# Layer 1 of a routed MLP in batches of four: seven products with 256 streamed columns instead of fourteen with 128

## The chip, the cores and the metric

The kernel runs on one core of a Trainium2 chip. Time is device time in microseconds (us) of one execution, of which the median over runs counts. The engines have short names in the profile: PE (TensorE, matmuls), PEld (its weight loads), DVE (VectorE), ACT (ScalarE), POOL (GpSimd) and SP (SyncE, which here only issues DMAs).

## The reference: what is computed

Attention with pooled queries for 8 batches of 8 heads, and then, in each batch, an MLP on the 128 tokens that score highest:

```python
q_pool = q.reshape(B, H, S // 2, 2, D).mean(axis=3)           # 8, 8, 576, 64
scores = q_pool @ k.transpose / sqrt(D); attn = softmax(scores)
x = (attn @ v) as (B, 576, 512)
scores = x @ w_gate
for b in range(B):
    top = the 128 tokens of batch b with the highest scores
    h = np.maximum(x[b, top] @ w1, 0.0)          # 512 -> 1024
    ye = h @ w2                                  # 1024 -> 512
    out[b, top] = x[b, top] + sigmoid(scores[b, top])[:, None] * ye
```

All of it is in float32.

## The kernel before, in words

The attention is one long loop of 64 half pairs (a pair is two heads of one batch, a half is 288 of its queries), and PE alternates between scores (`scores`, L878) and weighted values (`weighted`, L896). The other engines sum the exponentials, divide, multiply by `w_gate` and store the rows `x`.

In each batch a generator, `routed`, picks the tokens. Its steps are: add the parts of the scores (`line`, L1076, DVE), collect and add them up (`side_by_side` on ACT, `added` on DVE), write the row to DRAM and read it back shifted (L1088 and L1091, SP), compare every token's score with all others (L1116, DVE, ten instructions on `pick`), write the ranks to DRAM and read them back as a table (L1139 and L1143, SP), search in it for the tokens' numbers (L1152, DVE), gather their rows (L1179, a POOL DMA) into `xe`, and turn the gathered rows by way of DRAM (L1191 and L1209, SP) and a DVE transposition (L1216) into `xeT`, features on partitions. A `yield` stands between the steps, and the caller decides behind which other work each step is issued. Each engine takes its instructions in the order in which the code issues them.

The MLP of all batches is done behind the attention, in `ending` (L1383). Batches go in pairs, each pair in four stages. Two batches' tokens are taken as the two block rows of one matrix, the weight as 2 x 2 blocks, and each layer is done in seven block products instead of eight, with sums of blocks ahead of and behind them:

- `input_sums` (L1250): four sums of input blocks on POOL, 256 columns each (2 feature chunks of 128 tokens).
- `first_layer` (L1291): seven products of layer 1. `product(1, ...)` (L1263, matmuls at L1270) does one: eight matmuls, in each of which the weight block of 128 x 128 is stationary and the 128 tokens of one batch are streamed. Behind each product stand an ACT copy, or DVE adds (`add`, L1289) and a ReLU on ACT (L1303), 512 columns each. `u` and `w` are its two running sums.
- `four_sums` (L1344): four sums of blocks of the hidden layer on DVE, at L1351.
- `second_of` (L1353): seven products of layer 2 (matmuls at L1280; the tokens are stationary and 256 columns of the weight are streamed), adds on DVE, the gated residual (`scaled`, L1284), and `written` (L1238), which scatters a batch's rows to the output by a DMA of POOL.

The last pair's layer 2 is written out by hand in `ending`, with batch 7's scatter ahead of batch 6's.

The order of `ending` is this. Its first lines finish the attention. Batch 6's routing is under way (the generator `old`), batch 7's begins there (`new`). Then come the four pairs: layer 1, layer 2, layer 1, and so on. The steps that are left of `old` and `new` are issued by `pieces` (L1390): it counts the pieces of the MLP, of which each product is one, and before the pieces whose number is in `behind` it issues one step of the routing. So a step stands on its engines behind the work of the piece before.

Memory is taken over from the attention: `exponents_room`, `values_room` and `sums_room` are its buffers of exponentials, values and sums. PSUM is a pool of four buffers of two banks each (`banks`, L1063); they are handed out in turn, for products of either layer alike, so that a product waits until the work behind the fourth product before it has read its buffer.

Of the kernel before, what the change touches and what calls it, by code (L numbers as in the profile page):

```python
# [11 lines left out]
P = 128  # L12
# [3 lines left out]
F32 = mybir.dt.float32  # L16
# [524 lines left out]
class _Plain:  # L541
# [524 lines left out]
    def routed(self, b, part):  # L1066
# [16 lines left out]
        n = P - 1 + Sp  # L1083
# [61 lines left out]
        for s0, w in self.slots:  # L1145
# [27 lines left out]

            yield True
            if b == self.B - 1:
                xe = self.late[:, self.Dm : 2 * self.Dm]
# [16 lines left out]
            )  # L1193
            if b != self.B - 2:
                search(lines[:, :, 1, :], own_gate)
            if b < self.paired:
                xeT = ffn.tile([P, self.ND, P], F32, name="xeT", bufs=self.paired)
            else:
                xeT = self.lines_of((self.early if b < self.B - 1 else self.late)[:, 0 : self.Dm])
            yield True  # L1200
            moved = []

            def read():
                if b == self.B - 2:
                    moved.append(self.early[:, self.Dm : 2 * self.Dm])
                else:
                    room = ffn.tile([P, NT, P], F32, name="pick", bufs=1)
                    moved.append(room.rearrange("p t n -> p (t n)")[:, 0 : self.Dm])
                nc.sync.dma_start(moved[0], copy.rearrange("a (j b) m -> (a j) (b m)", b=n))  # L1209

            if b < self.B - 2:
# [8 lines left out]
            token = {"xe": xe, "xeT": xeT, "gate": own_gate, "index": index, "rows": rows_out, "w": w, "b": b}  # L1220
            self.tokens.append(token)

    def part_of_rows(self, token, part, parts):
# [36 lines left out]
    def lines_of(self, room):  # L1260
        return room.rearrange("p (c n) -> p c n", n=P)

    def product(self, layer, of, by, to):  # L1263

        n = of.shape[1]
        if layer == 1:
            to = self.lines_of(to)[:, :, 0 : of.shape[2]]
            for f in range(by.shape[2] // P):
                for k in range(n):
                    self.nc.tensor.matmul(  # L1270
                        to[:, f, :],
                        lhsT=by[:, k, f * P : (f + 1) * P],
                        rhs=of[:, k, :],
                        start=k == 0,
                        stop=k == n - 1,
                    )
        else:
            to = to[0 : of.shape[2], 0 : by.shape[2]]
            for k in range(n):
                self.nc.tensor.matmul(to, lhsT=of[:, k, :], rhs=by[:, k, :], start=k == 0, stop=k == n - 1)  # L1280
        return to

    def scaled(self, to, of, token, plus):
        self.nc.vector.scalar_tensor_tensor(  # L1284
# [5 lines left out]

    def first_layer(self, a, s, c, m):  # L1291

        copy = self.nc.scalar.copy
# [4 lines left out]
        def product(of, by):  # L1298
            return self.product(1, of, by, self.banks()[:, 0, :])

        def hidden(to, x, y):
            self.add(to, x, y)
            self.nc.scalar.activation(to, to, AF.Relu)  # L1303

        copy(u, product(a11, b11))
        yield
        hidden(c11, u, product(a12, b21))
        yield
        copy(w, product(s1, t1))
        yield  # L1310
        self.add(u, u, product(s2, t2))
        self.add(w, w, u)
        yield
        ps = product(s3, t3)
        hidden(c22, w, ps)
        self.add(u, u, ps)
        yield
        hidden(c21, u, product(a22, t4))
        yield
        hidden(c12, w, product(s4, b22))  # L1320
        yield

    def second_layer(self, a, s, order):

        (a11, a12, _, a22), (s1, s2, s3, s4) = a, s
        b11, b21, b22 = (self.quarter(2, i, j) for i, j in ((0, 0), (1, 0), (1, 1)))
        t1, t2, t3, t4 = self.last_sums
        products = (a11, b11), (a12, b21), (s1, t1), (s2, t2), (s3, t3), (s4, b22), (a22, t4)
        for i in order:
            yield self.product(2, *products[i - 1], self.banks()[:, 0, :])  # L1330
# [5 lines left out]
    def quarters_of(self, tiles, w):  # L1336

        n = tiles[0].shape[1] // 2
        return [tile[:, i * n : (i + 1) * n, 0:w] for tile in tiles for i in range(2)]
# [13 lines left out]
    def second_of(self, tokens, a, s, y):  # L1353

        copy, add = self.nc.scalar.copy, self.add
        half, w = self.Dm // 2, tokens[0]["w"]
        y1, y2, y7, y3, y4 = (y[0:w, i * half : (i + 1) * half] for i in range(5))
        to = [token["xe"][0:w, i * half : (i + 1) * half] for token in tokens for i in range(2)]
        one, two = tokens
        products = self.second_layer(a, s, (1, 2, 7, 3, 4, 5, 6))  # L1360
        for part in (y1, y2, y7):
            copy(part, next(products))
            yield
        copy(y3, next(products))
# [12 lines left out]
        for of, at, token in ((y3, to[1], one), (y4, to[2], two), (y7, to[3], two)):  # L1377
            self.scaled(at, of, token, at)
        for token in tokens:
            self.written(token, token["index"])  # L1380
        yield

    def ending(self, halves, old):  # L1383

        nc, half, copy = self.nc, self.Dm // 2, self.nc.scalar.copy
        last = halves[-1]["pair"]
        n, w = self.NFC * P, self.tokens[0]["w"]
        done, behind = 0, (8, 9, 10, 11, 15, 16, 17, 18, 23, 28, 29, 31, 32, 38)

        def pieces(unit, n=None):  # L1390
            nonlocal done
            for i, _ in enumerate(unit):
                if done in behind:
                    next(waiting)
                done += 1
                if i + 1 == n:
                    break

# [6 lines left out]
        def sums_room():  # L1405
            return self.row(self.work.tile([P, G, 2 * self.HALF], F32, name="acc"))

        def layers(i, room, m):
            tokens = self.tokens[2 * i : 2 * i + 2]
            c = self.quarters_of([self.lines_of(room[:, k * n : (k + 1) * n]) for k in range(2)], w)  # L1410
            s = self.lines_in(room[:, 2 * n : 4 * n], self.NFC // 2, w, 4)
            a = self.quarters_of([token["xeT"] for token in tokens], w)
            sums = self.lines_in(room[:, 4 * n :], self.ND // 2, w, 4)
            return tokens, c, s, (a, sums), self.first_layer(a, sums, c, m)

        self.early = values_room()
        rooms, acc = [exponents_room()], [sums_room(), sums_room()]
        m = [self.lines_in(acc[0], 4, w, 2)]
        m.append(self.lines_in(self.load.tile([P, self.S], F32, name="kT"), 4, w, 2))
        following = layers(0, rooms[0], m[0])  # L1420

        self.gated(halves[-3])
        next(old)
        self.weighted(halves[-1])
        self.drained(halves[-1])
        self.multiplied(halves[-2])
        self.input_sums(*following[3])
        self.multiplied(halves[-1])
        self.scored(halves[-3])
        self.gated(halves[-2])  # L1430
        self.late = values_room()
        rooms.append(exponents_room())
        pieces(following[4], 1)
        self.normalized(last)
        self.gated(halves[-1])
        self.scored(halves[-1])
        _, new, _ = self.routing.pop()
        waiting = chain((None for _ in old), (None for _ in new), count())
        pieces(following[4], 1)
        for of in (halves[-3]["pair"], last):  # L1440
            self.divided(of)
            self.stored(of)

        for i in range(1, self.B // 2):
# [10 lines left out]
        (six, seven), c, s, _, third = following  # L1455
        pieces(third, 3)
# [225 lines left out]
```

## Time and profile before

| What | us |
|---|---|
| Median of 3 runs (674.3 to 675.34) | 674.61 |
| The profiled execution's own time | 675.29 |
| Its span, first to last instruction | 673.6 |
| PE busy in the span | 665.6 |
| First product of layer 1 starts on PE | 568.67 |
| First product of the last pair's layer 2 starts | 655.65 |
| Last scatter is issued | 668.76 |

Times in the profile's views are us from the span's start, so the last 105 us of the table are the MLP. A line of the timeline has start, length, engine, line in the code, operation, output and input with their shape, the number of instructions, and in square brackets how long the engine was idle before and what it waited for. fp32 matmuls have two records each on PE, so that the eight matmuls of a layer 1 product are shown as x16. The granted TensorE clock is 1.0.

Of the stretches between 568.7 and 643.0 (columns: busy us of each engine with the number of instructions, PE's clock, DMA share, GB/s):

```profile
568.70:593.80 25.10, 25.10 (x176) 23.58 (x173) 16.66 (x34) 6.97 (x17) 8.90 (x11) 1.00 0.25 53
593.80:618.40 24.60, 24.60 (x170) 23.02 (x169) 18.20 (x46) 5.25 (x11) 5.54 (x8) 1.00 0.19 64
618.40:643.00 24.60, 24.60 (x171) 23.09 (x170) 15.07 (x28) 5.18 (x10) 6.06 (x7) 1.00 0.17 55
```

The order is PE, PEld, DVE, ACT, POOL. PE has no idle time in any of the three, and DVE is busy for two thirds to three quarters.

### The profile page before, as it was taken

The numbers are of one execution on the slowest core, as the hardware profiler recorded it, in microseconds if no ns is written. First come the engines' busy times: TensorE is split into PE (matmuls) and PEld (weight loads), VectorE is DVE, ScalarE is ACT, GpSimd is POOL, SyncE is SP. The second block draws the span as 40 slices with busy tenths as digits, with TensorE's granted clock in tenths as the row PEclk, the third lists the DMA queues.
The fourth block names the chain that finished last, engine by engine and source line by source line (L and its number), as shares of the span: only waits on it lengthen the run. The fifth ranks groups of instructions, "written<-read, shape, count | busy, mean of one in ns | idle before, by whom it ended". The sixth has DMA issues, their size and how long they took to land.

```text
span 673.6 us, 23393 instructions
## 1 busy us (share of the span) xinstructions
PE 665.6 (99%) x9939; PEld 445.6 (66%) x9939; DVE 571.8 (85%) x825; ACT 446.0 (66%) x973; POOL 502.0 (75%) x473
## 2 busy tenths in 40 slices
PE   8999999999999999999999999999999999999996
PEld 5656666666666666666666666656666666999995
DVE  3878999999999987998899889988898898777564
ACT  6667778777777777777777777777777775212210
POOL 5788888889888988899888978897889877312211
PEclk9999999999999999999999999999999999999999
DMA  8798988877987689868966788688868745211201
GB/s 160 132 206 183 171 198 185 179 127 156 175 151 127 118 160 156 164 115 172 170 116 129 150 164 147 128 155 154 149 128 156 146 132 152 52 54 56 63 32 36
DMA packets 391049, 92.69 MB, mean 138 GB/s; under 512 B 371608, under 2 KB 376088, under 8 KB 390936
## 3 DMA queue, kind: packets, MB, share of 16 engines
q1 hardware_dynamic: 389496, 86.73, 66.7%
q0 software_dynamic: 1280, 4.20, 1.7%
q8 instruction: 79, 1.29, 0.8%
q14 instruction: 34, 0.28, 0.2%
q10 hardware_dynamic: 160, 0.20, 0.1%
HBM read 75.30 MB, written 15.79 MB: 135 GB/s over the span
## 4 chain that ended last, share of the span: by engine, by line
PE 92%; SPq 3%; issue 2%; DMA 2%; POOL 1%; DVE 0%; POOLq 0%
PE ps L896 40%; PE ps L878 39%; PE ps L1270 7%; PE ps L1280 5%; SPq L741 1%; DMA v_sb<-in_v_dram 1%; SPq L735 1%; DMA qb<-in_q_dram 1%; SPq L802 0%; DMA out_dram<-v_sb,index 0%; POOL acc L917 0%; SPq L794 0%; POOL qp L763 0%; POOL out_dram L1241 0%; SPq L811 0%
## 5 line engine op out<-in xcount | busy, mean ns | idle before, releaser
L885 ACT ACTIVATE p<-ps 128x576 f32<-128x576 f32 x576 | 320.5, 698 | 2.2 <-PE ps L878 1.9
L917 POOL TENSOR_TENSOR acc<-p 128x576 f32<-128x576 f32 x192 | 281.6, 1493 | 36.3 <-ACT p L885 35.3
L878 PE MATMUL ps<-qT,kT 64*64 64x288 f32 x4608 | 292.0, 403 | 0.1
L896 PE MATMUL ps<-p,v_sb 64*64 64x288 f32 x4608 | 291.0, 403 | 0.5 <-DMA v_sb<-in_v_dram 0.5
L896 PEld LDWEIGHTS ps<-p,v_sb 64*64 64x64 f32 x4608 | 173.5, 133 | 106.9 <-ACT p L885 15.6
L878 PEld LDWEIGHTS ps<-qT,kT 64*64 64x64 f32 x4608 | 174.3, 133 | 105.2 <-ACT p L885 13.5
L922 DVE TRANSPOSE_TENSOR_REDUCE fold<-p 128x54 f32<-128x1728 f32 x64 | 126.2, 1972 | 40.6 <-ACT p L885 40.6
L904 ACT COPY two<-ps 128x576 f32<-128x576 f32 x64 | 40.9, 638 | 133.2 <-PE ps L896 133.2
L922 DVE TRANSPOSE_TENSOR_REDUCE fold<-acc 128x54 f32<-128x1728 f32 x64 | 124.5, 1945 | 3.8 <-POOL acc L917 3.7
L906 POOL TENSOR_TENSOR av<-two 128x288 f32<-128x288 f32 x64 | 51.3, 802 | 39.2 <-ACT two L904 38.2
L766 DVE STREAM_TRANSPOSE kT<-kb 128x1152 f32<-128x1152 f32 x31 | 74.4, 2399 | 0.0
L985 POOL TENSOR_TENSOR prod<-avb,w_gate 128x288 f32<-128x288 f32 x64 | 52.5, 821 | 0.0
L763 POOL TENSOR_TENSOR qp<-qb 128x576 f32<-128x576 f32 (+1 forms) x32 | 43.8, 1370 | 6.1 <-DMA qb<-in_q_dram 5.1
L1116 DVE TENSOR_SCALAR_CACHE_REDUCE pick<-line 128x127 f32<-128x127 f32 (+4 forms) x80 | 45.1, 564 | 2.2
L962 ACT ACTIVATE sums<-total,tiny 32x18 f32<-32x18 f32 x124 | 38.2, 308 | 2.0
L1021 POOL TENSOR_TENSOR x<-avb,rec 128x576 f32<-128x576 f32 x30 | 34.8, 1160 | 0.0
L1241 POOL DMA_INDIRECT out_dram<-xe,index x7 | 7.0, 1007 | 35.1 <-DVE xe L1284 27.5
L1303 ACT ACTIVATE p<-p 128x512 f32<-128x512 f32 x16 | 10.1, 631 | 34.1 <-DVE p L1289 32.0
L975 DVE STREAM_TRANSPOSE avb<-av 128x288 f32<-128x288 f32 x64 | 28.4, 443 | 3.9 <-POOL av L906 3.9
L1043 DVE TENSOR_REDUCE red<-prod 128x9 f32<-128x288 f32 x64 | 27.8, 435 | 2.7 <-POOL prod L985 2.7
L947 ACT COPY groups<-sum 32x36 f32<-32x36 f32 x124 | 27.2, 219 | 2.4 <-DVE sum L932 0.8
L771 DVE STREAM_TRANSPOSE qT<-qp 128x576 f32<-128x576 f32 (+1 forms) x32 | 23.6, 736 | 0.8 <-POOL qp L763 0.8
(113 smaller groups left out, 436.3 us busy)
## 6 DMA issues: line engine op xcount, KB each, us to landing
kb<-in_k_dram SPq DMA_DIRECT2D x124, 144.0 KB, 4.7
qb<-in_q_dram SPq DMA_DIRECT2D x124, 144.0 KB, 4.7
v_sb<-in_v_dram SPq DMA_DIRECT2D x31, 576.0 KB, 5.5
out_dram<-x SPq DMA_DIRECT2D x128, 72.0 KB, 5.0
lines<-row_rank SPq DMA_DIRECT2D x8, 640.0 KB, 4.8
w<-in_moe_w_dram SPq DMA_DIRECT2D x8, 512.0 KB, 5.7
line<-gate_lines SPq DMA_DIRECT2D x8, 351.5 KB
tw<-tw SPq DMA_DIRECT2D x4, 512.0 KB, 7.6
```

What stands on the lines that cost most here:

```text
L763: nc.gpsimd.tensor_tensor(out=qp[:, of, :], in0=pair["q"][:, of, 0, :], in1=pair["q"][:, of, 1, :], op=ALU.add)
L766: nc.vector.transpose(kT.rearrange("p (c i g) -> p c g i", c=self.NC, i=BLK), pair["k"].rearrange("p (g c) d -> p c g d", c=self.NC),)
L878: nc.tensor.matmul(sc[keys, j, 0:n], lhsT=pair["kT"][rows, c * P + keys.start : c * P + keys.stop], rhs=pair["qT"][rows, qs], start=True, ...
L885: nc.scalar.activation(p[:, c // G, c % G, :, :], sc[:, :, 0:n], AF.Exp, scale=self.scale)
L896: nc.tensor.matmul(av[j * self.D : (j + 1) * self.D, e, 0:n], lhsT=half["pair"]["v"][keys, j, c, :], rhs=half["p"][keys, c // G, c % G, j, :],
L904: nc.scalar.copy(two[:, :, :], av[:, :, 0:n])
L906: nc.gpsimd.tensor_tensor(out=half["av"][:, :], in0=two[:, 0, :], in1=two[:, 1, :], op=ALU.add)
L917: nc.gpsimd.tensor_tensor(out=acc[:, u, :], in0=units[:, 0, u, :], in1=units[:, 1, u, :], op=ALU.add)
L922: nc.vector.tensor_reduce(fold[:, a, :], of.rearrange("p u (m d) -> p (u m) d", d=BLK), AX.X, ALU.add, apply_transpose=True,)
L985: self.nc.gpsimd.tensor_tensor(out=pair["prod"][:, ns, :], in0=pair["avb"][:, ns, :], in1=self.w_gate[:, hp : hp + 1, :].broadcast_to([P, ...
L1116: nc.vector.tensor_scalar(out=cmp[0:rows, 0 : part.stop - part.start], in0=near[0:rows, part], scalar1=sc[0:rows, t : t + 1], scalar2=None ...
L1270: self.nc.tensor.matmul(to[:, f, :], lhsT=by[:, k, f * P : (f + 1) * P], rhs=of[:, k, :], start=k == 0, stop=k == n - 1,)
```

## The change

Layer 1 is done for four batches at a time. The block rows of its matrix are two pairs of batches, so that a matmul streams 2 x 128 tokens; there are two rounds of seven products instead of four. A product fills both banks of a PSUM buffer (1024 columns), and the sums, ReLUs and copies of layer 1 have 1024 columns instead of 512, the input sums 512 instead of 256. Layer 2 stays as it is, pair by pair, with two of them behind each round of layer 1. The order of the products in layer 1 changes (`s2 t2` and `s1 t1` change places, `s4 b22` comes fifth instead of last), and one copy is gone.

All of batch 6's and 7's inputs are needed in the second round, at its start. So the steps of their routing are issued earlier among the products: `behind` has other numbers, a layer 1 product counts as two pieces, and batch 6's read (L1209) is issued ahead of the stores of `x`. Batch 6's gathered rows are turned in `pick`. The `xeT` of two batches lie in one tile, the input sums in a buffer of sums and in one of keys. The scatters move behind the work that follows (`scattered`).

```diff
-            if b < self.paired:
-                xeT = ffn.tile([P, self.ND, P], F32, name="xeT", bufs=self.paired)
-            else:
-                xeT = self.lines_of((self.early if b < self.B - 1 else self.late)[:, 0 : self.Dm])
+            if b % 2 == 0:
+                if b < self.paired:
+                    self.turned = ffn.tile([P, 2, self.ND, P], F32, name="xeT", bufs=self.paired // 2)
+                else:
+                    self.turned = self.early.rearrange("p (t c n) -> p t c n", t=2, n=P)
+            turned, xeT = self.turned, self.turned[:, b % 2]
...
             def read():
-                if b == self.B - 2:
-                    moved.append(self.early[:, self.Dm : 2 * self.Dm])
-                else:
-                    room = ffn.tile([P, NT, P], F32, name="pick", bufs=1)
-                    moved.append(room.rearrange("p t n -> p (t n)")[:, 0 : self.Dm])
+                room = ffn.tile([P, NT, P], F32, name="pick", bufs=1)
+                moved.append(room.rearrange("p t n -> p (t n)")[:, 0 : self.Dm])
...
+    def first_product(self, of, by):
+
+        n = of.shape[2]
+        to = self.banks().rearrange("p b (f t n) -> p (b f) t n", t=2, n=P)[:, :, :, 0 : of.shape[3]]
+        for f in range(by.shape[2] // P):
+            for k in range(n):
+                self.nc.tensor.matmul(
+                    to[:, f],
+                    lhsT=by[:, k, f * P : (f + 1) * P],
+                    rhs=of[:, :, k, :],
+                    start=k == 0,
+                    stop=k == n - 1,
+                )
+        return to
...
-        copy(u, product(a11, b11))
+        self.nc.scalar.copy(u, product(a11, b11))
         yield
         hidden(c11, u, product(a12, b21))
         yield
-        copy(w, product(s1, t1))
+        add(u, u, product(s2, t2))
         yield
-        self.add(u, u, product(s2, t2))
-        self.add(w, w, u)
+        add(w, u, product(s1, t1))
+        yield
+        hidden(c12, w, product(s4, b22))
         yield
         ps = product(s3, t3)
         hidden(c22, w, ps)
-        self.add(u, u, ps)
+        add(u, u, ps)
         yield
         hidden(c21, u, product(a22, t4))
-        yield
-        hidden(c12, w, product(s4, b22))
         yield
...
-        done, behind = 0, (8, 9, 10, 11, 15, 16, 17, 18, 23, 28, 29, 31, 32, 38)
+        done, behind = 2, (3, 4, 5, 9, 10, 11, 12, 13, 18, 19, 21, 22, 27)
...
-        self.input_sums(*following[3])
+        rooms.append(exponents_room())
+        a, c, layer = first(0)
+        self.input_sums(a, inputs)
         self.multiplied(halves[-1])
         self.scored(halves[-3])
         self.gated(halves[-2])
         self.late = values_room()
-        rooms.append(exponents_room())
-        pieces(following[4], 1)
+        next(old)
+        next(layer)
...
-        pieces(following[4], 1)
         for of in (halves[-3]["pair"], last):
             self.divided(of)
             self.stored(of)
-
-        for i in range(1, self.B // 2):
-            tokens, c, s, _, layer = following
-            pieces(layer)
-            second = self.second_of(tokens, c, s, acc[1])
-            pieces(second, 1)
-            self.four_sums(c, s)
-            pieces(second, 3)
-            following = layers(i, rooms[i % 2], m[i % 2])
-            self.input_sums(*following[3])
-            pieces(second)
...
+        pieces(layer, 4, 2)
+        x, y = second(0, 0, c), second(0, 1, c)
+        self.four_sums(*x[1:])
+        pieces(layer, of=2)
+        layer = self.second_of(*x, acc[1])
+        pieces(layer, 3)
+        self.four_sums(*y[1:])
+        pieces(layer)
+        self.scattered(x[0])
+        pieces(self.second_of(*y, acc[1]))
+        a, c, layer = first(1)
+        self.input_sums(a, inputs)
+        self.scattered(y[0])
+
+        pieces(layer, 2)
         low = self.counted()
-        pieces(third, 2)
+        pieces(layer, 2)
         outside = self.outside(low)
-        pieces(third, 1)
-        self.four_sums(c, s, slice(0, 3))
-        pieces(third)
-        self.four_sums(c, s, slice(3, 4))
-
+        pieces(layer, 1)
+        x, y = second(1, 0, c), second(1, 1, c)
+        self.four_sums(*x[1:])
+        pieces(layer)
+        layer = self.second_of(*x, acc[1])
+        pieces(layer, 3)
+        self.four_sums(*y[1:])
+        pieces(layer)
+        self.scattered(x[0])
```

In it `first(i)` gives round i's input blocks, hidden blocks and its generator of products; `second(i, j, c)` gives pair j of round i its tokens, hidden blocks and room for their sums. `pieces(layer, n, of)` issues n products, each of which counts `of` pieces.

More of the change, by code (lines that the diff above doesn't have):

```diff
@@ L1175, in routed @@
             if b == self.B - 1:
-                xe = self.late[:, self.Dm : 2 * self.Dm]
+                xe = self.late[:, 0 : self.Dm]
             else:
@@ L1219, in routed @@
             )
-            token = {"xe": xe, "xeT": xeT, "gate": own_gate, "index": index, "rows": rows_out, "w": w, "b": b}
+            token = {"xe": xe, "turned": turned, "gate": own_gate, "index": index, "rows": rows_out, "w": w, "b": b}
             self.tokens.append(token)
@@ L1261, in lines_of, with hidden_of, second_product, scattered @@
         return room.rearrange("p (c n) -> p c n", n=P)
-    def product(self, layer, of, by, to):
-        n = of.shape[1]
[L1266 to L1280, printed above, removed]
-        return to
+    def hidden_of(self, room, w):
+        return room.rearrange("p (f t n) -> p f t n", t=2, n=P)[:, :, :, 0:w]
+    def first_product(self, of, by):
[11 more added lines that the diff above has]
+        return to
+    def second_product(self, of, by):
+        n = of.shape[1]
+        to = self.banks()[0 : of.shape[2], 0, 0 : by.shape[2]]
+        for k in range(n):
+            self.nc.tensor.matmul(to, lhsT=of[:, k, :], rhs=by[:, k, :], start=k == 0, stop=k == n - 1)
+        return to
+    def scattered(self, tokens):
+        for token in tokens:
+            self.written(token, token["index"])
     def scaled(self, to, of, token, plus):
@@ L1291, in first_layer @@
     def first_layer(self, a, s, c, m):
-        copy = self.nc.scalar.copy
         (a11, a12, _, a22), (s1, s2, s3, s4), (c11, c12, c21, c22), (u, w) = a, s, c, m
@@ L1296, in first_layer @@
         t1, t2, t3, t4 = (self.summed(1, i) for i in range(4))
-        def product(of, by):
-            return self.product(1, of, by, self.banks()[:, 0, :])
+        product, add = self.first_product, self.add
         def hidden(to, x, y):
@@ L1329, in second_layer @@
         for i in order:
-            yield self.product(2, *products[i - 1], self.banks()[:, 0, :])
+            yield self.second_product(*products[i - 1])
     def row(self, tile):
@@ L1334, in row @@
         return tile.rearrange(f"p {names} -> p ({names})")
-    def quarters_of(self, tiles, w):
-        n = tiles[0].shape[1] // 2
-        return [tile[:, i * n : (i + 1) * n, 0:w] for tile in tiles for i in range(2)]
     def lines_in(self, room, n, w, count):
@@ L1378, in second_of @@
             self.scaled(at, of, token, at)
-        for token in tokens:
-            self.written(token, token["index"])
         yield
@@ L1386, in ending, with pieces @@
         last = halves[-1]["pair"]
-        n, w = self.NFC * P, self.tokens[0]["w"]
-        done, behind = 0, (8, 9, 10, 11, 15, 16, 17, 18, 23, 28, 29, 31, 32, 38)
-        def pieces(unit, n=None):
+        w = self.tokens[0]["w"]
+        n = self.NFC // 2 * 2 * P
+        done, behind = 2, (3, 4, 5, 9, 10, 11, 12, 13, 18, 19, 21, 22, 27)
+        def pieces(unit, n=None, of=1):
             nonlocal done
             for i, _ in enumerate(unit):
-                if done in behind:
-                    next(waiting)
-                done += 1
+                for _ in range(of):
+                    if done in behind:
+                        next(waiting)
+                    done += 1
                 if i + 1 == n:
@@ L1406, in sums_room, with first, second @@
             return self.row(self.work.tile([P, G, 2 * self.HALF], F32, name="acc"))
[L1408 to L1416, printed above, removed]
+        def first(i):
+            x, y = (self.tokens[4 * i + 2 * j]["turned"] for j in range(2))
+            a = [t[:, :, k * self.ND // 2 : (k + 1) * self.ND // 2, 0:w] for t in (x, y) for k in range(2)]
+            c = [self.hidden_of(rooms[i][:, k * n : (k + 1) * n], w) for k in range(4)]
+            m = [self.hidden_of(room[:, 4 * n : 5 * n], w) for room in rooms]
+            return a, c, self.first_layer(a, inputs, c, m)
+        def second(i, j, c):
+            a = [c[2 * j + k][:, :, t, :] for t in range(2) for k in range(2)]
+            s = self.lines_in(rooms[1 - i][:, 2 * j * n : 2 * (j + 1) * n], self.NFC // 2, w, 4)
+            return self.tokens[4 * i + 2 * j : 4 * i + 2 * j + 2], a, s
+        self.early = values_room()[:, 0 : 2 * self.Dm]
         rooms, acc = [exponents_room()], [sums_room(), sums_room()]
-        m = [self.lines_in(acc[0], 4, w, 2)]
-        m.append(self.lines_in(self.load.tile([P, self.S], F32, name="kT"), 4, w, 2))
-        following = layers(0, rooms[0], m[0])
+        inputs = [acc[0][:, i * 2 * half : (i + 1) * 2 * half] for i in range(3)]
+        inputs.append(self.load.tile([P, self.S], F32, name="kT")[:, 0 : 2 * half])
+        inputs = [room.rearrange("p (t c n) -> p t c n", t=2, n=P)[:, :, :, 0:w] for room in inputs]
         self.gated(halves[-3])
@@ L1442, in ending @@
             self.stored(of)
-        for i in range(1, self.B // 2):
-            tokens, c, s, _, layer = following
-            pieces(layer)
-            second = self.second_of(tokens, c, s, acc[1])
-            pieces(second, 1)
-            self.four_sums(c, s)
-            pieces(second, 3)
-            following = layers(i, rooms[i % 2], m[i % 2])
-            self.input_sums(*following[3])
-            pieces(second)
-        (six, seven), c, s, _, third = following
-        pieces(third, 3)
+        pieces(layer, 4, 2)
[12 more added lines that the diff above has]
+        pieces(layer, 2)
         low = self.counted()
-        pieces(third, 2)
+        pieces(layer, 2)
         outside = self.outside(low)
-        pieces(third, 1)
-        self.four_sums(c, s, slice(0, 3))
-        pieces(third)
-        self.four_sums(c, s, slice(3, 4))
+        pieces(layer, 1)
[7 more added lines that the diff above has]
+        self.scattered(x[0])
+        (six, seven), c, s = y
         to = [token["xe"][0:w, i * half : (i + 1) * half] for token in (six, seven) for i in range(2)]
```

## The prediction

> **What bounds the kernel now.** I read the page's busy shares first, then the chain of waits, then the timelines of PE, DVE, POOL and SP over the last 110 us.
>
> ```profile
> PE 665.6 (99%) x9939; PEld 445.6 (66%) x9939; DVE 571.8 (85%) x825; ACT 446.0 (66%) x973; POOL 502.0 (75%) x473
> ...
> 568.74 1.98 PE ps L1270 x16
> 570.73 0.15 PE ps L998 x2
> 570.87 10.80 PE ps L1270 x96
> 581.67 12.09 PE ps L1280 x56
> 593.76 12.50 PE ps L1270 x112
> 606.26 12.14 PE ps L1280 x56
> 618.40 12.50 PE ps L1270 x112
> 630.91 12.09 PE ps L1280 x56
> 643.00 8.94 PE ps L1270 x80
> ...
> 665.25 0.98 POOL L1241 DMA_INDIRECT out_dram<-v_sb,index  x1 [16.49 <-DVE v_sb L1284]
> 668.76 0.97 POOL L1241 DMA_INDIRECT out_dram<-xe,index  x1 [2.53 <-DVE xe L1284]
> ```
>
> PE is busy 99%, and the chain (columns: start, length, what) runs on PE through the whole tail: a product of the MLP that ends sooner brings the end forward, a PE stall puts it back. Everything before 568.7 us stays as it is: no engine's order changes ahead of it. From the first product of the last layer 2 (655.65) to the span's end is 17.95 us; its order is kept.
>
> ```profile
> 574.78 0.45 DVE L1043 TENSOR_REDUCE red<-prod 128x9 f32<-128x288 f32 x1 [2.69 <-POOL prod L985]
> ...
> 575.99 2.07 DVE L1021 TENSOR_TENSOR x<-avb,rec 128x576 f32<-128x576 f32 x2
> 577.98 0.67 DVE L1289 TENSOR_TENSOR acc<-acc,ps 128x512 f32<-128x512 f32 x1
> ...
> 576.88 5.31 SPq L1032 DMA_DIRECT2D out_dram<-x  x8
> ...
> 593.29 0.33 SPq L1091 DMA_DIRECT2D line<-gate_lines  x1
> ```
>
> In the traffic view from 591 to 599 (tenths of the DMA engines' time in 40 slices of 0.2 us):
>
> ```profile
> DMA  0000000001000000467977441000998400000000
> ```
>
> DVE and SP hold what may become late: batch 7's gate row goes through `red`, the `x` products, eight stores on SP, then two small DMAs. Of these the traffic view shows the second, issued at 593.29, in the slices from 594.2 to 596.0 (what follows is a scatter).
>
> [...]
>
> **The change part by part.**
>
> PE. Layer 1 now: 28 products x 1.786 us = 50.0. After: [...]14 x 3.457 = 48.4. Gain 1.6. No row of before streams two batches through a strided 256: lower price 3.457 (L1280's row)[...]; a price of 3.57 (nothing saved) is the worst I allow. I take 3.457, since its row streams 256 fp32 columns too. Layer 2: 28 products of 1.729 before and after, nothing. The merge matmul (0.15) and the count's (0.12) stay.
>
> So, unstalled, PE runs: products 1 to 7 from 568.84 (with the merge) to 593.19, layer 2 of batches 0, 1 to 605.29, of 2, 3 to 617.4, second layer 1 to 641.7, layer 2 of 4, 5 to 653.8; against 655.65 that is 1.85, of which 0.2 are small gaps of the first stages that I leave in: 1.6.
>
> POOL. The input sums become 4 instructions of 512 elements. L1258's 256 cost 0.72, L985's 288 cost 0.79, L917's 576 cost 1.40: 2.05 ns an element, so 1.25 each; chained: 571.10, 572.43, 573.63, 574.83, ending at 576.08 (1.33 apart where one reads the other's result, 1.20 where not, as the rows of 256 show with 0.80 and 0.69). The second sum, needed by product 3 at 575.9, is ready at 573.7: covered by 2.2. The last `prod` (L985), behind them, ends at 576.83 instead of 574.75: `red` and its followers start 2.1 later. L1021's `x` starts 577.48 instead of 575.99 (before, a `hidden` sum stood ahead of it).
>
> SP. Batch 6's read (L1209) is issued ahead of the eight stores; its source lands by 572.2 (2.3 after the copy, as at 630.43 to 632.76), so it holds nobody. The stores run 578.4 to 583.7; batch 7's gate row follows at 583.8 (DVE's `total` is ready at 583.2), the line read 1.34 later, as at 591.95 to 593.29: 585.1. The traffic view shows the line's bytes moving until 2.7 us after its issue; with 0.3 to 0.6 for the stores ahead I take the line as landed at 588.3.
>
> DVE. The adds on 1024 columns: 512 cost 0.69, 256 cost 0.42, so 1.23, spacing 1.15. 14 of these stand for 28 of 512 columns, so the work falls slightly, which no one waits for; what counts is order. Add for product 5 at 586.3 to 587.5, two memsets to 587.7; the comparisons then wait for the line at 588.3: two comparisons 1.25, four sums 2.54, two wide adds 2.3, four comparisons 2.32, the add of product 7 at 1.2: 9.6 us, done 597.9. This last add frees the PSUM buffer that the fourth product of layer 2 needs at 593.19 + 3 x 1.729 = 598.4. Cover 0.5 us; when it is gone, every 1 us costs 1.
>
> The next such place: the search (L1152) in front of the adds for product 6 of layer 2. From 597.9: four comparisons and the rank 2.45, its DMA pair 1.45 between issues, then the table read, whose bytes in the same view from 612 on move until 3.3 after issue (614.07 to 617.3): 3.5. So 605.4; the search 1.5, two adds 0.8: 607.7, and PE needs that buffer at 608.7. Cover 1.0. If the read takes 4.8, as once in the loop (555.72 to 560.5), it is late by 0.3.
>
> Batch 7's chain: index 606.9, gather 3.6 to the copy, 2.3 to the read, 2.7: landed at 615.8; DVE reaches the transposition at 619.1, ends 620.3, the two first sums end at 623.0, and product 3 needs them at 624.3. Cover 1.3. Scatters of 4, 5 start 1.3 and 4.8 after 653.8 and the second lands 3.5 on, at 662.1; batch 7's own scatter comes 9.6 after it, 663.4. Cover 1.3. ACT's work on 1024 columns (1.06 by the 512 and 256 rows) follows DVE and meets no PE wait: at product 5 of layer 2 its copy must free a buffer within 1.73 us of the same late add, and needs 1.7.
>
> Edits with one answer, at nothing: the fourth sum in `kT` waits for the last scores, over at 568.7, and its turn is at 574.8; batch 6's row in `pick` is transposed at 581.7, 6 us ahead of batch 7's comparisons, which write there; `xeT` in pairs and the earlier second room issue no instruction. The count (L1499, 1.5 us of DVE) stands between adds of the second layer 1 that come 3.46 us apart and take 1.15, so it fits.
>
> Sum: 673.6 - 1.6 = 672.0 us of span. The profiled execution took 675.29, 0.68 above the median of the three runs; so 674.61 - 1.6 = 673.0.
>
> **Rivals.**
>
> A, the forecast, chance 0.50: 1.6 gained, all covers hold: 673.0; 672.4 to 673.3 with noise.
>
> B, chance 0.28: a PSUM buffer takes the place of the PE time. The cover of 0.5 is the smallest and hangs on one landing; with the line at 589.3, PE waits 0.5, with 589.8 1.0; the table read adds up to 0.9 in its place. For it: DVE stays behind PE from 588 to 599. Against: the traffic view's 2.7. Takes 0.3 to 1.5: 673.8.
>
> C, slower, chance 0.12: the gate row queues behind the stores. In the loop the row and its line took 534.23 to 537.26 to 541.74 (POOL waited for it), 7.5 us. From 583.8 that is 591.3, 2.5 beyond the 588.8 that PE bears; 2.5 - 1.6 = 0.9 slower: 675.5. It decides from a landing at 590.4 on. Against: the loop's key and value loads, which shared those microseconds, are gone; it needs both delays.
>
> D, chance 0.10: the change does what it says, but 256 strided columns cost twice 128: [...] Against: that row.
>
> **How the numbers follow.** The measurement can't tell less than about 0.2%, 1.35 us, from no change. A is faster by 0.24%: 0.50. B and D, and a little of C, lie within: 0.40. Slower: 0.10. The range reaches from A's lower end, 672.4, to B's and D's upper ends, 674.6, which leaves C and the tails out.
>
> **What would show it.** Product 3.46 us apart on PE, 16 records of 216 ns. `red` at 576.9, line read at 585.1, the add of product 7 ended by 598.4, no gap on PE at 598 or 608. The last layer 2 starts at 654.0. The forecast is wrong if the matmul records are longer than 218 ns, or PE shows gaps of over 0.3 us after 593.

## The result, and the profile after

Over 13 runs each, the changed kernel takes 673.42 us (672.76 to 673.65) and the kernel before 674.5 us (674.28 to 675.53): a ratio of 0.998, with a 95% interval from 0.9972 to 0.9989. That is about 1.1 us gained of 1.6 forecast; the interval reaches from 0.7 to 1.9. The profiled execution has a span of 671.9 us, where 672.0 was forecast, but 0.25 of that is luck: its first product of layer 1 starts at 568.42 instead of 568.67, although nothing had been changed ahead of it. In the other profiles below that start lies anywhere from 567.5 to 568.6. So I compare stretches: from the start of layer 1's first product to that of the last layer 2's second product (the first product that stands on a line of its own in all traces).

The two ends of the stretch in the kernel before (timeline of PE):

```profile
568.67 2.05 PE L1270 MATMUL ps<-xeT,w 128*128 128x128 f32 x16
...
657.38 1.89 PE L1280 MATMUL ps<-kb,p 128*128 128x256 f32 x8
```

And the timeline of PE in the changed kernel (layer 1 is L1271 here, layer 2 L1285):

```profile
568.42 3.72 PE L1271 MATMUL ps<-xeT,w 128*128 128x256 f32 x16
571.98 0.31 PE L998 MATMUL ps<-sum,merge 128*128 128x36 f32 x2
572.12 3.70 PE L1271 MATMUL ps<-xeT,w 128*128 128x256 f32 x16
575.66 7.07 PE L1271 MATMUL ps<-acc,tw 128*128 128x256 f32 x32
582.57 3.62 PE L1271 MATMUL ps<-kT,w 128*128 128x256 f32 x16
586.02 3.62 PE L1271 MATMUL ps<-acc,tw 128*128 128x256 f32 x16
589.47 3.62 PE L1271 MATMUL ps<-xeT,tw 128*128 128x256 f32 x16
592.92 3.62 PE L1285 MATMUL ps<-w,p 128*128 128x256 f32 x16
596.38 1.89 PE L1285 MATMUL ps<-kT,p 128*128 128x256 f32 x8
598.30 1.99 PE L1285 MATMUL ps<-kb,p 128*128 128x256 f32 x8
600.13 1.89 PE L1285 MATMUL ps<-qb,p 128*128 128x256 f32 x8
...
608.76 1.89 PE L1285 MATMUL ps<-kT,p 128*128 128x256 f32 x8
610.49 1.89 PE L1285 MATMUL ps<-kb,p 128*128 128x256 f32 x8
...
655.70 1.89 PE L1285 MATMUL ps<-kb,p 128*128 128x256 f32 x8
```

A product of layer 1 starts 3.45 us after the one before it (582.57, 586.02, 589.47), 216 ns a record. The stretch is 655.70 - 568.42 = 87.28 us; in the kernel before it was 657.38 - 568.67 = 88.71. So the MLP brought 1.43. There is one gap of note: `kT` at 596.38 runs 1.73 us, to 598.11, and `kb`, the fourth product of layer 2, starts at 598.30. The product behind the gap then takes 1.83 us instead of 1.73 (598.30 to 600.13), so that PE loses 0.3 us at this place in all; the same 0.1 stands behind the gaps in e3 (`kb`, 600.73 to 602.56) and e4 (`qb`, 612.15 to 613.98) below, 1.83 each. What `kb` waited for stands in the timeline of DVE of the changed kernel (in brackets the idle time and what ended it):

```profile
576.68 0.45 DVE L1043 TENSOR_REDUCE red<-prod 128x9 f32<-128x288 f32 x1 [2.74 <-POOL prod L985]
577.17 0.18 DVE L1052 TENSOR_TENSOR part<-red,rec 128x18 f32<-128x18 f32 x1
577.35 1.43 DVE L1021 TENSOR_TENSOR x<-avb,rec 128x576 f32<-128x576 f32 x2
...
588.74 0.35 DVE L1116 TENSOR_SCALAR_CACHE_REDUCE pick<-line 128x127 f32<-128x127 f32 x1 [1.15 <-DMA line<-gate_lines]
...
597.03 1.22 DVE L1298 TENSOR_TENSOR p<-p,ps 128x1024 f32<-128x1024 f32 x1
...
606.88 1.34 DVE L1152 SCALAR_TENSOR_TENSOR pick<-lines,token,token_line 128x640 f32<-128x640 f32 x1 [1.39 <-DMA lines<-row_rank]
...
608.34 1.27 DVE L1298 TENSOR_TENSOR acc<-acc,ps 128x256 f32<-128x256 f32 x3
```

DVE stood idle until the line landed at 588.74, and the add that reads product 7 of layer 1 (at 597.03) ended at 598.25, 0.14 behind the time at which PE wanted its buffer. The end, finally, is as before: batch 7's scatter 9.6 us after the last layer 2 began, the last one 3.5 behind it (timeline of POOL, changed kernel):

```profile
663.57 0.98 POOL L1240 DMA_INDIRECT out_dram<-v_sb,index  x1 [3.70 <-DVE v_sb L1293]
667.06 0.98 POOL L1240 DMA_INDIRECT out_dram<-xe,index  x1 [2.52 <-DVE xe L1293]
```

### The profile page after: what moved, and what is told of

The parts are those of the page before. It is cut to its first block, busy times and chain, and to the rows that moved or that the text cites. A ratio compares the mean times of both kernels' runs of the same rounds, so it can differ in the third digit from the quotient of the medians.

```text
span 671.9 us, 22869 instructions
## 1 busy us (share of the span) xinstructions
PE 665.1 (99%) x9715; PEld 438.4 (65%) x9715; DVE 565.2 (84%) x811; ACT 441.2 (66%) x959; POOL 499.8 (74%) x465
## 4 chain that ended last, share of the span: by engine, by line
PE 92%; issue 5%; DMA 2%; POOL 1%; DVE 0%; POOLq 0%
PE ps L878 42%; PE ps L896 42%; PE ps L1285 4%; PE ps L1271 4%; DMA out_dram<-xe,index 1%; PE ps L623 1%; DMA out_dram<-v_sb,index 0%; POOL acc L1257 0%; POOL out_dram L1240 0%; PE ps L844 0%; DVE xe L1293 0%; POOL kT L1257 0%; DVE v_sb L1215 0%; PE ps L830 0%; DVE acc L1298 0%
## 5 line engine op out<-in xcount | busy, mean ns | idle before, releaser
L1309 ACT ACTIVATE p<-p 128x1024 f32<-128x1024 f32 x8 | 8.5, 1058 | 39.0 <-DVE p L1298 33.5
L1298 DVE TENSOR_TENSOR p<-p,ps 128x1024 f32<-128x1024 f32 x14 | 16.9, 1216 | 11.9 <-PE ps L1271 11.8
```

## The experiments

Two theories were to be told apart. W: the gain is the streaming width alone (1.6 us), less a gap on PE at a place where the routing of batch 7 has become late. O: the new order and the half as many ACT and DVE instructions carry part of it. Then each of the covers that the prediction had worked out (a cover is the time by which something may come later before PE waits for it) was taken away in turn. Stretches are of the profiled execution; the kernel before has 88.71 and the changed one 87.28.

| Run | Change against the changed kernel | Median, us | Ratio to the kernel before | Stretch, us |
|---|---|---|---|---|
| e1_width_128 | two matmuls of 128 columns | 674.87 | 1.0005 (0.9997 to 1.0013) | 89.01 |
| e2_row_first | gate row ahead of the stores | 673.14 | 0.998 (0.9971 to 0.9988) | 86.98 |
| e3_line_late | line read twice | 676.85, one run | | 90.80 |
| e4_table_late | rank table read twice | 673.93, one run | | 88.46 |
| e5_prod_first | `prod` ahead of the sums | 673.41 | 0.9976 (0.9967 to 0.9985) | 86.98 |
| e6_both | e2 and e5 | 673.22 | 0.9974 (0.9963 to 0.9985) | 86.98 |
| e7_rows_late | rows read three times | 679.74, one run | | 92.93 |
| a1_after_again | none | 673.26 | 0.9978 (0.9969 to 0.9987) | 87.03 |
| e9_row_first_again | as e2 | 673.1 | 0.9976 (0.9966 to 0.9985) | 86.97 |
| e8_rows_twice | rows read twice | 674.26, one run | | 87.82 |

The kernel before took 674.47 us beside e1 to e4, 675.2 beside e5 to e7 and 674.62 beside the last three, so that ratios and stretches are to be compared, not medians from different groups.

**e1: the width alone.**

```diff
         for f in range(by.shape[2] // P):
-            for k in range(n):
-                self.nc.tensor.matmul(to[:, f], lhsT=..., rhs=of[:, :, k, :], ...)
+            for t in range(2):
+                for k in range(n):
+                    self.nc.tensor.matmul(to[:, f, t], lhsT=..., rhs=of[:, t, k, :], ...)
```

> The changed kernel with every layer 1 matmul of 2 x 128 columns split into two of 128, nothing else. Theory W (the gain is the streaming width alone): a layer 1 product takes 3.57 us instead of 3.455, 14 of them 1.6 us; PE then comes 0.35 us later to the buffer at which it waits 0.19 us in the changed kernel, so that gap goes, and the whole is 1.4 us slower than the changed kernel: the time of the kernel before within 0.3 us. Theory O (the new order and the fewer, wider DVE and ACT instructions carry part of the gain): at least 0.5 us faster than the kernel before although its matmuls are as narrow.

With narrow matmuls the whole gain is gone: the ratio's interval holds 1, and the stretch is 1.73 longer than the changed kernel's. The products are 3.57 apart, twice the 1.79 of the kernel before. O falls: with order, pairs and wide sums in place nothing is faster. In one point the expectation was wrong: the gap on PE didn't go. In this execution SP's eight stores took 6.44 us instead of 5.31, the line landed later too (at 588.89, 21.21 us after the first product of layer 1, instead of 20.32), and PE waited 0.25. With the slower product behind it (598.45 to 600.28, 1.83) that is 0.35 us, which accounts for the 0.30 by which the stretch is longer than that of the kernel before (the median is 0.4 longer, where at most 0.3 was expected). One thing e1 doesn't separate: it halves the columns of a matmul and doubles the number of matmuls at once (a product has x32 records instead of x16), and with them the weight loads, as the kernel before does (9939 records of PEld on its page, 9715 on the changed kernel's), so "width" stands for both.

**e2, e5 and e6: the gap.** e2 lets two more products, and with them the gate row of batch 7, go ahead of the stores of both pairs:

```diff
         for of in (halves[-3]["pair"], last):
             self.divided(of)
-            self.stored(of)
-        pieces(layer, 4, 2)
+        pieces(layer, 2, 2)
+        for of in (halves[-3]["pair"], last):
+            self.stored(of)
+        pieces(layer, 2, 2)
```

e5 puts POOL's multiplication ahead of its four input sums, and e6 is both:

```diff
-        self.input_sums(a, inputs)
         self.multiplied(halves[-1])
+        self.input_sums(a, inputs)
         self.scored(halves[-3])
```

> The changed kernel with the eight stores of x on SP issued behind batch 7's gate row and its read instead of ahead of them. If the stores set when the line lands: the row is issued at 582.5 instead of 583.5, the line lands at about 586.7 instead of 588.74, the comparisons start at the end of the memsets (587.6), the add for product 7 ends at 597.1 and PE's gap of 0.19 us before the fourth product of layer 2 is gone: 0.2 us faster than the changed kernel, all else the same. If another wait holds the line (the DMA pair itself), the landing moves by under 1 us and the gap stays.

> The changed kernel with POOL's last gate product (prod) ahead of the four input sums of the first round instead of behind them. If the wide sums are what makes batch 7's gate row late: red starts 5 us earlier, the x products 2 us earlier (they then meet the add for product 2), the stores end 2 us earlier, the line lands at about 586.7 in the changed kernel's times, the gap of 0.19 us on PE before the fourth product of layer 2 goes, and the second input sum comes 0.8 us later, still 0.7 us ahead of product 3: 0.2 us faster than the changed kernel. If the stores on SP hold the row whatever POOL does, nothing changes.

> Both orders in one: prod ahead of the sums, and the gate row ahead of the stores. The gap is gone with either alone, so the two together bring no more than one: the same 0.2 us against the changed kernel (673.1 to 673.3), with the line landing 2 to 4 us ahead of its use. If DVE's queue behind the line, and not its landing, held PE's buffers elsewhere too, the two together would be faster than either.

All three have the same stretch, 86.98, 0.30 below the changed kernel's, and no gap. In e2 the line had landed before DVE came to it (at 586.31, by POOL's wait for it; counted from the first product of layer 1, 1.5 us earlier than in the changed kernel, where 2.0 were expected). In e5 POOL's order alone did it, with the stores in their old place; the line still came 0.41 behind DVE, within what PE bears. It came only 0.8 us earlier there, not 2: `red` was ready 2.8 us earlier, but the two `x` products behind it took 2.56 us instead of 1.43 (last section). e6 brings nothing on top, as said: once the line is early enough, no other wait of these is left on PE. Its line landed 1.3 us ahead of its use, not 2 to 4. In the time none of this is to be seen: the ratios lie within one another's intervals.

**a1 and e9: the same two kernels side by side.**

> The changed kernel itself, beside the next kernel on the same chip. Theory W (width less one gap): 1.0 to 1.6 us faster than the kernel before, PE's stretch from the first product of layer 1 to the first of the last layer 2 85.4 to 85.7 us, with a gap of 0.1 to 0.3 us before the fourth product of the first layer 2. If part of the first measured gain was the start of the run and not the change, the stretch is longer than 86 us.

> The kernel with the gate row ahead of the stores, again, beside the changed kernel: the same stretch without the gap, 85.25 us, and a time 0.2 to 0.3 us below the changed kernel's. If the two medians agree within 0.1 us or stand the other way, a gap of 0.2 us is not to be seen in the time of this kernel.

The changed kernel is 1.36 us below the kernel before here, and e9 is 0.16 below the changed one: less than was expected, with intervals that overlap. The reason stands in the trace: in this execution of the changed kernel the gap was as good as gone (product 4 at 597.45, where product 3 ended; 0.05 before the next), and its stretch, 87.03, is that of e9 but for 0.06. (The expectations end the stretch one product earlier: 85.30 and 85.24 in their count, so the first is below the 85.4 that I had set as its lower end.) Three more runs, e4, e7 and e8, are the same as the changed kernel up to this point. The table has, for all of them, when the line landed, counted from the start of the first product of layer 1, and what PE lost between the first and the fifth product of layer 2, which stand 6.91 us apart where nothing waits. With them stand e5 and the next experiment, e3.

| Run | Line lands after, us | PE loses, us |
|---|---|---|
| e5_prod_first | 19.56 | 0 |
| e8_rows_twice | 20.06 | 0.04 |
| a1_after_again | 20.06 | 0.05 |
| e7_rows_late | 20.12 | 0.11 |
| e4_table_late | 20.26 | 0.24 |
| the changed kernel | 20.32 | 0.30 |
| e3_line_late | 23.28 | 3.26 |

From about 20.0 us on, what the line comes later is lost by PE, one for one. The changed kernel has a cover of about zero, and the landing of one DMA decides on which side of it an execution falls.

**e3: the line late.** The line's read is made twice for batch 7, the second behind the first on the same tile.

```diff
-            nc.sync.dma_start(near[:, 0:n], _next_of(row[0:n], P))
+            for _ in range(2 if b == self.B - 1 else 1):
+                nc.sync.dma_start(near[:, 0:n], _next_of(row[0:n], P))
```

> The changed kernel with batch 7's shifted line read twice, the second read behind the landing of the first: the line lands about 3.4 us later, at 592.1. If the cover is used up (theory of the prediction): the add for product 7 ends 3.4 us later, PE waits some 3.5 us before the fourth product of layer 2 and the span grows by 3.3 to 3.5 us, one for one. If DVE has slack behind the line that the sum of its rows hides, the growth is under 2 us.

The stretch grew by 3.52. But PE doesn't wait at one place, and the line was not 3.4 us late (a line of the timeline of DVE, then of PE, e3):

```profile
591.17 0.34 DVE L1117 TENSOR_SCALAR_CACHE_REDUCE pick<-line 128x127 f32<-128x127 f32 x1 [4.12 <-DMA line<-gate_lines]
...
592.39 3.62 PE L1286 MATMUL ps<-w,p 128*128 128x256 f32 x16
597.28 1.97 PE L1286 MATMUL ps<-kT,p 128*128 128x256 f32 x8 [1.27 <-issue]
600.73 1.99 PE L1286 MATMUL ps<-kb,p 128*128 128x256 f32 x8 [1.49 <-DVE p L1299]
...
611.65 1.99 PE L1286 MATMUL ps<-kT,p 128*128 128x256 f32 x8 [0.29 <-DVE acc L1299]
```

The two products at 592.39 end at 595.85, so PE waits 1.43 before `kT`, some 1.6 between its end (599.1, as it stands behind a gap) and `kb`, and 0.46 later, before 611.65. The buffer of layer 1's product 6, read by two adds that also stand behind the comparisons, came first, then that of product 7. DVE's wait for the line grew from 1.15 to 4.12 us: it was 2.96 later than in the changed kernel, and at these two places PE lost 2.96 more (3.26 against 0.30). That price is one for one, as said. The rest of the growth, 0.56 with the slower product, comes at 611.65, where the product waited for the adds behind the search: that is the prediction's second cover (e4, next). So the sum of 3.5 agrees with the expectation by chance: the line was less late, and a second wait was added.

**e4: the table late.** The same with the read of the rank table.

```diff
-        nc.sync.dma_start(lines.rearrange("p i a t -> p (i a t)"), _rows_of(row[:], P))
+        for _ in range(2 if b == self.B - 1 else 1):
+            nc.sync.dma_start(lines.rearrange("p i a t -> p (i a t)"), _rows_of(row[:], P))
```

> The changed kernel with batch 7's rank table read twice: it lands about 3.7 us later, at 610.6, so that the adds for product 6 of the first pair's layer 2 end at 612.8. As the prediction had it, the third product of the second pair waits for that buffer and stands at PE from 608.76 on: a gap of 4.0 us there. If, as the trace of the changed kernel suggests (that product started at 608.76 while those adds ran until 609.1), the buffer is that of the fourth product, wanted at 610.49: a gap of 2.3 to 2.6 us there, none at the third, and a span longer by 2.3 to 3.2 us, the last part if batch 7's rows then come late for the second round.

```profile
609.90 1.34 DVE L1153 SCALAR_TENSOR_TENSOR pick<-lines,token,token_line 128x640 f32<-128x640 f32 x1 [5.32 <-DMA lines<-row_rank]
...
612.15 1.99 PE L1286 MATMUL ps<-qb,p 128*128 128x256 f32 x8 [0.69 <-DVE acc L1299]
```

Both sides were wrong about the place and the size: the search waited until 609.90, the adds for product 6 followed at 611.36, and PE had one gap of 0.85 before the *fifth* product of the second pair (wanted at 611.30, started at 612.15) and one of 0.17 in the second round. The stretch grew by 1.18. The programs show why. PSUM buffers aren't strictly handed out in turn. In the kernel before they are, as far as the MLP goes; in the changed kernel the third product of the second pair takes the buffer of that pair's first product, which ACT's copy frees early (607.28 to 607.65 in its trace), and so passes over that of product 6; the program of e4 passes over it twice. The order is fixed when the program is made, and moves with small changes: e2, e3 and e6 hand the buffers out in turn again, which is why e3's third product, at 611.65, waited for product 6's adds. So this run measured another hand-out along with the late table.

**e7 and e8: batch 7's rows late.** e7 makes the read of the rows three times; e8 has a 2 in the place of the 3.

```diff
-                nc.sync.dma_start(moved[0], copy.rearrange("a (j b) m -> (a j) (b m)", b=n))
+                for _ in range(3 if b == self.B - 1 else 1):
+                    nc.sync.dma_start(moved[0], copy.rearrange("a (j b) m -> (a j) (b m)", b=n))
```

> The changed kernel with batch 7's turned rows read three times, each behind the landing of the one before: they land at about 623.7 instead of 618. By the prediction's cover (the landing may be as late as 620.5, 1.3 us behind DVE's turn at 619.25), PE waits 3.2 to 3.5 us before the third product of the second round, and the span grows by as much. If the second input sum is needed later than the rows show, the growth is under 2 us.

> The changed kernel with batch 7's turned rows read twice: they land about 3.1 us later than in it, at 621.2, 0.7 us behind what PE bears. A gap of 0.6 to 0.9 us before the third product of the second round, and no more: with three reads the gap of 4.06 us was followed by 3 us at half the clock, which cost another 1.8; if that is the price of a long gap, a short one has none (clock 1.0 behind it). If the clock falls behind any gap at this place, the growth is twice the gap or more.

With two reads the rows landed at 620.61, PE waited 0.68 (wanted at 623.89, started at 624.57), and the stretch is 87.82: the 86.98 without gaps, plus that wait, plus some 0.1 for the slower products behind the gap (7.11 us from 624.57 to the count's matmul at 631.68, where the changed kernel has 7.00) and 0.04 at the line. With three they landed at 624.39 and PE waited 4.06, but the stretch grew by 5.65. The two waits, e8 first (timeline of PE):

```profile
624.57 7.17 PE L1272 MATMUL ps<-acc,tw 128*128 128x256 f32 x32 [0.53 <-POOL acc L1258]
...
628.32 8.86 PE L1272 MATMUL ps<-acc,tw 128*128 128x256 f32 x32 [3.89 <-POOL acc L1258]
```

The view of stretches by engine for e7, PE alone (columns: busy us with records, granted clock, DMA share, GB/s), shows the rest:

```profile
617.35:624.26 6.91, 6.91 (x33) 1.00 0.42 117
624.26:628.32 4.06, 0.17 (x2) 1.00 0.00 0
628.32:631.80 3.48, 3.48 (x9) 0.57 0.00 0
631.80:633.80 2.00, 2.00 (x10) 0.89 0.34 131
633.80:637.20 3.40, 3.40 (x18) 1.00 0.20 77
```

In 3.48 us behind the gap PE did 9 records instead of 16, at a clock of 0.57. From 628.32 to the count's matmul at 637.11 it took 8.79 us, where the changed kernel has 7.00 (624.30 to 631.30); the other 1.8 us are that. The expectation of e7 (3.2 to 3.5) had the landing 0.7 too early and didn't have the clock. In e8, and in e3 with two gaps of 1.4 and 1.6, the clock stayed at 1.00.

## Why the prediction was right, point by point

- **The gain on PE.** Forecast 14 x 3.457 against 28 x 1.786: 1.6. The 3.457 is twice the 1.729 us that a product of layer 2, four matmuls of 256 columns, took in the kernel before. The products came at 3.45 (216 ns a record; the 218 ns that the forecast set as its limit were the author's own choice), and e1 took the width away and with it all of the gain. Where no gap stands (e2), the stretch is 1.73 shorter than before: the walk along PE had 1.85, and the 0.2 of small gaps that it left in was nearer 0.1. This matmul with a strided stream of two batches costs what L1280's did (eight of them 3.45 us, against 3.46); rival D, for which it would have been twice 1.786, 3.57, falls.
- **The first cover** (0.5 us, the add for product 7). The mechanism was right, and the size off by 0.65: it was -0.14. The term that failed is the DMA pair behind the stores. I had 1.34 us from the row to the line's read and 3.2 to its landing; it was 1.77 and 3.43. The stores ahead explain the first: in e2 and e6, where they come behind, it is 1.33. They don't explain the second, which is 3.43 in e2 too, and 3.17 in a1; why it varies is not shown. DVE was earlier than summed, since the two `x` products took 1.43 instead of 2.07, but this didn't help, because the row waited for SP's stores. So the forecast, A, came with a small piece of B, a loss of 0.3 us in the profiled execution and of 0.05 in a1; the 673.42 lies just above A's 673.3.
- **The second cover** (1.0 us, the search). Here a step failed: "PE needs that buffer at 608.7". The adds for product 6 ended at 609.1 and that product started at 608.76 all the same, since it took another buffer; the one in question was wanted at 610.49. The table was 1.5 us later than summed (606.88 instead of 605.4; 2.3 between its two DMAs instead of 1.45), which would have cost 0.3 at the place that I had in mind. The true cover was 1.4. So two errors cancelled, the late table and the buffer that I had wrong, and that no gap came here is luck: in e3, whose program hands the buffers out in turn, it came. Why the table's two DMAs are 2.3 apart, with no stores ahead of them, is not shown.
- **Batch 7's rows** (cover 1.3). DVE reached the transposition at 619.25 without a wait, the second sum was done at 623.2, product 3 wanted it at 624.3: 1.1. e8 confirms it: the rows came 1.70 behind DVE's turn and PE waited 0.68, so 1.0 was covered. The landing itself was summed too early (615.8; the terms as written give 615.5): the rows were read at 615.04 and came at about 618 (an estimate: in e7 and e8 one such read takes 2.6 to 3.1 us), since the table was late, and this was hidden behind DVE.
- **POOL and SP.** The wide sums took 1.26 each (1.25 forecast), `red` came at 576.68 (576.9), the stores ran from 578.13 (578.4), and the read of the line was issued at 585.31 (585.1).
- **Rival C** (slower by a late line). Not what happened, but its price is right: in e3 the line came 3.3 us later than PE bears (23.28 against some 20.0 in the table above), and PE lost 3.26 there, more than the change brings.

Forecast 673.0, measured 673.42. The 0.4 us between them is less than the interval. In the profiled execution the gap cost 0.3; how much it cost in the others, which have no trace, is not shown, and in the traces of the same code it ranges from 0.04 to 0.30.

## What to carry to other kernels

Doubling the columns that a matmul streams took 3% off the products concerned here (3.57 to 3.45 us); work such a gain out first from the durations at both widths, since it is an upper limit, and then look for what the larger unit needs earlier. Bringing work together costs slack: each of the chains that fed the second half was moved up until its cover was about 1 us or none, and a cover is best listed with the one landing on which it hangs. Where one is near zero, moving an independent bulk transfer behind the small one that others wait for (e2), or a short instruction ahead of long ones on its engine (e5), gives it back for nothing (0.3 us of the stretch here, too little to see in the medians). And where the cover hangs on which buffer a product gets, look it up in the program instead of counting in turn.

## What the runs showed of the hardware that was not expected

- A gap of 4.06 us on PE was followed by some 3.4 us at half the clock, which added 1.8 us to its price (e7); gaps of 0.7 to 1.6 us had no such price, with the clock at 1.00 behind them (e3, e8). In slices of 1 us from 628.3 the granted clock in e7 was 0.76, 0.50, 0.50, 0.53 and then 1.00, from which the 3.4 us are estimated. For gaps between 1.6 and 4.06 us these runs show nothing, and what sets the length of the slow stretch is not shown either.
- Some operations of DVE took longer while POOL was at its sums. In e5 the product `part` of 18 elements took 1.19 us, nearly as long as one of POOL's sums (1.27), and the two `x` products 2.56 (timeline of DVE, e5):

```profile
574.38 1.19 DVE L1052 TENSOR_TENSOR part<-red,rec 128x18 f32<-128x18 f32 x1
575.49 2.56 DVE L1021 TENSOR_TENSOR x<-avb,rec 128x576 f32<-128x576 f32 x2
```

  `part` ended as POOL's third sum did (574.26 to 575.53). With POOL idle, as in the changed kernel above, the same two lines are 0.18 and 1.43. The reduction `red`, which reads `prod` alone, was not held up by a sum that ran beside it (0.39 at 573.95, e5). What makes the difference is not shown: no run was made to test it. The 2.07 that the prediction took for the two `x` products was measured in such a moment, too: in the kernel before POOL was at its sums from 574.71 to 578.65, and two of them took 1.25 us instead of 0.72.
